# Attention and FFN on one core: conversions behind SiLU in batch 0, and small matmuls gathered behind FFN1 from batch 1 on

## The chip, the cores and the metric

The kernel runs on one core of one Trainium2 chip. The metric is device time in microseconds of one execution, as the median of several. The engines are named as the profile names them: PE is TensorE (matmuls) and PEld its weight loads, DVE is VectorE, ACT is ScalarE, SP issues most of the DMAs.

## What is computed

Eight batches of an attention over 32 memory slots, followed by a feed-forward layer over all 4608 tokens. Cut to what matters:

```
q, k, v: (8, 8, 576, 64)   phi: (8, 8, 576, 32)   w_in: (512, 2048)   w_out: (2048, 512)
a    = exp(phi - max over seq);  a = a / (sum over seq + 1e-9)
k_m  = einsum('bhsm,bhsd->bhmd', a, k);   v_m = the same with v
attn = softmax(q @ k_m^T / 8)                      # over the 32 slots
x    = (attn @ v_m) put together over heads        # (4608, 512)
h    = x @ w_in;   g = h * sigmoid(h);   out = g @ w_out
```

## The kernel before, in words

**Precision.** The large products are made of pairs of a high part and a low part, each of a type that the PE takes quickly (fp32r): high by high, high by low, low by high. So each large product is three matmuls. Splitting a value is a copy to the high part and a subtraction for the low part.

**Order of the algebra.** `attn @ v_m @ w_in` is computed as attn times P, where P = `v_m @ w_in` for one batch (`p_mm`, L560 to L578, matmuls at L570). P is made in four pieces of 512 columns of d_ff (eight of 256 in batch 0), each in the PSUM tile `bg`; `p_split` (L580) then writes its high part on ACT (L584) and its low part on DVE (L586).

**Slots.** For each batch b there are 16 slots, one for each 128 columns of d_ff (`fc`). A slot is: FFN1 (`ffn1`, L590, 12 matmuls at L605) into the PSUM tile `h`; SiLU on ACT (`silu`, L628 for 512 of the 576 tokens, L630 for the other 64, which go to `gleft`); the split of g on DVE (L620 and L622); and FFN2 of the slot before (`ffn2`, 12 matmuls at L642, four tiles of tokens by three parts). The tile `h` has two banks, of which FFN1 uses columns 0 to 287 in each. There is one `h`, so the next FFN1 waits until SiLU has read it. After every second batch the 64 left tokens of two batches go through FFN2 together (`accleft`, `left_step`).

**Attention of the next batch** is done meanwhile, step by step, as events hung on the slots (L672 to L718). Its steps: the maximum of phi (`phi_max`, then `phi_fold`, DVE), the subtraction (`phi_sub`, L294 and L297, DVE), the exponential (`phi_exp`, L301, ACT, with a table load before it and another before the next SiLU); `e_mm` (L315 and L323, small matmuls into `bg`, then reciprocals and `kvn` on DVE and ACT); `e_tr` (the turn: two transposes at L349 and two copies to `kvT`); `s_mm` (the scores in two halves of 288 tokens, small matmuls at L361 into `bg`, turned on DVE at L373); maximum, subtraction, exponential (L395), sum and norm of the scores; `s_back` and `s_low`, which turn them back and split them. In batches 1 to 6 these hang on the slots

```
mx, sub, ex, em, tr, s0, s1, sx, se, ss, sn, sk = 0, 1, 2, 3, 4, 6, 7, 8, 9, 10, 11, 12
```

and P on slots 1, 5 and 9, with the next batch's first piece in slot 14. In a slot the program issues two tiles of FFN2 (six matmuls), then the events of the slot, then the other six, then the events of the half slot (L845 to L848).

**Batch 0** also converts the weights, which arrive as 64-bit words. `w_conv` (L146) has the steps p, c and h on ACT (L166, L168, L174) and s, a and l on DVE (L170, L172, L176); l makes `wo_lo`. The conversions are events of the slots as well. Three buffers hold the raw words.

**What sets the order.** The Tile framework orders the instructions of each engine by priority, which follows the program, and inserts the waits. `in_order` (L98) forces program order on the engines that it names: PE, SP, DVE and ACT in the opening, PE and SP up to the end of batch 0 (`whole`, closed at L836). From batch 1 on no engine is bound by it. In the opening (L729 to L816) batch 0's attention is done by hand, with `keep_warm` matmuls in the gaps; `f_copy` copies scores out of PSUM, whole on ACT or in halves on ACT and DVE, and `f_high` and `f_low` split the result.

Of the kernel before, what the change touches and what calls it, by code (L numbers as in the profile page):

```python
# [10 lines left out]
F32 = mybir.dt.float32  # L11
# [4 lines left out]
AF = mybir.ActivationFunctionType  # L16
# [32 lines left out]
def attn_ffn_kernel(  # L49
# [64 lines left out]
    def bgtile():  # L114
        return ps.tile([P, 2, 512], F32, tag="bg", name="bg", bufs=1)

    raws, cvas = {}, {}

    def w_load(w, part=None, few=False):

# [23 lines left out]
    def w_conv(w, part=None, steps="pcsahl"):  # L146


        kind, j = w
        words = raws[w].bitcast(U32).rearrange("p r (f t) -> p r f t", t=2)  # L150
        low, high = (w_part(words[:, :, :, t], part) for t in range(2))
        r = low.bitcast(I32)
        fc = slice(2 * j, 2 * j + 2) if part is None else slice(2 * j + part, 2 * j + part + 1)
        if kind == "i":
            to = win[:, fc].rearrange("p k r f -> p k (r f)")
            a = to.bitcast(I32)
        else:
            to = high.bitcast(F32)
            if (w, part) not in cvas:
                n, tag = (2, "cva") if part != 1 else (1, "cva1")  # L160
                cvas[w, part] = sb.tile([P, n, DMODEL], I32, tag=tag, name="cva", bufs=1)[:, : 2 if part is None else 1]
            a = cvas[w, part]
        au = a.bitcast(U32)
        for step in steps:
            if step == "p":
                nc.scalar.activation(a.bitcast(F32), high.bitcast(F32), AF.Prelu, scale=2.0**-112, alpha=-(2.0**32))  # L166
            elif step == "c":
                nc.scalar.activation(r, low, AF.Copy, scale=2.0**-29)  # L168
            elif step == "s":
                nc.vector.tensor_scalar(au, au, 3, None, op0=ALU.logical_shift_left)  # L170
            elif step == "a":
                nc.vector.tensor_tensor(to.bitcast(I32), a, r, op=ALU.add)  # L172
            elif kind == "o" and step == "h":
                nc.scalar.activation(wo_hi[:, fc], a.bitcast(F32), AF.Copy)  # L174
            elif kind == "o":
                nc.vector.tensor_tensor(wo_lo[:, fc], to, wo_hi[:, fc], op=ALU.subtract)  # L176

    later = [w for j in range(2, DFF // CW) for w in (("i", j + 1), ("o", j))][:-2] + [("o", DFF // CW - 1)]
    to_load = iter([("i", 1), ("o", 1), ("i", 2)] + later)
# [19 lines left out]
    def banks(b):  # L199
        if b == 0:  # L200
            return [ps.tile([P, 512], F32, tag="acc", name=f"first{i}", bufs=NI) for i in range(2)]
        bg = bgtile()
        return [bg[:, 0], bg[:, 1]]

    def load_phi(b):
        t = sb.tile([P, PHW], F32, tag="att", name=f"phi{b}")
# [99 lines left out]

    def e_mm(b):
        e, er, kvt, kr = (at[b][k] for k in ("e", "er", "kv", "kr"))
        pt = banks(b)
        turns = [(c, p) for c in range(FULLC) for p in range(2)]  # L310
        if b == 0:
            turns.sort(key=lambda t: t[1])
        for c, p in turns:
            for r in range(NR):
                nc.tensor.matmul(  # L315
                    pt[p][M * r : M * (r + 1), :KVW],
                    e[:, p, c, M * r : M * (r + 1)],
                    kvt[c][:, p, r],
                    start=c == 0, stop=False, skip_group_check=True,
                )  # L320
        for r in range(NR):
            for p in range(2):
                nc.tensor.matmul(  # L323
                    pt[p][M * r : M * (r + 1), :KVW],
                    er[rows(p), M * r : M * (r + 1)],
                    kr[rows(p), r],
                    start=False, stop=True, skip_group_check=True,
                )
        rs = [sb.tile([P, 1], F32, tag="rs", name="rs", bufs=2) for p in range(2)]
        for p in range(2):  # L330
            nc.vector.tensor_scalar(rs[p], pt[p][:, 2 * D : KVW], EPS, None, op0=ALU.add)
        for p in range(2):
            nc.vector.reciprocal(rs[p], rs[p])
        for p in range(2):
            src = pt[p][:, : 2 * D].rearrange("p (k d) -> p k d", k=2)
            if p == (b == 0):
                nc.scalar.activation(kvn[:, :, p], src, AF.Copy, scale=rs[p])
            else:
                nc.vector.tensor_scalar(kvn[:, :, p], src, rs[p], None, op0=ALU.mult)  # L339

    def e_tr(b):
        if b > 1:
            bg = bgtile()
            pt = [bg[:, 0, P * kind : P * (kind + 1)] for kind in range(2)]
        else:
            pt = [live["h"][:, kind, HALF : HALF + P] for kind in range(2)]
        t = sb.tile([P, 2, NR, M], F32, tag="kvT", name=f"kvT{b}", bufs=2)
        for kind in range(2):
            nc.tensor.transpose(pt[kind], kvn[:, kind].rearrange("p g d -> p (g d)"), ident)  # L349
        nc.vector.tensor_copy(t[:, 0].rearrange("p r m -> p (r m)"), pt[0])  # L350
        nc.scalar.copy(t[:, 1].rearrange("p r m -> p (r m)"), pt[1])
        at[b]["kvT"] = t

    def s_mm(b, hf):
        if "sc" not in at[b]:
# [269 lines left out]
    def silu(b, fc, h):  # L625
        g32 = sb.tile([P, MAIN], F32, tag="g32", name="g32", bufs=2)
        w = MAIN // 2
        nc.scalar.activation(g32.rearrange("p (h f) -> p h f", h=2), h[:, :, :w], AF.Silu)  # L628
        o = b % 2 * LEFT
        nc.scalar.activation(  # L630
            gleft[:, fc, o : o + LEFT].rearrange("p (h f) -> p h f", h=2), h[:, :, w:HALF], AF.Silu
        )
        return g32

    acc = {}
# [39 lines left out]
        events.setdefault((b, slot), []).append((fn, a))  # L675

    for b in range(B):
        if b == 0:
            for j in range(2, DFF // CW):
                ev(b, 2 * j - 1.5, p_mm, b, j * CW, CW)  # L680
        else:
            for j in range(1, NJ):
                ev(b, 4 * j - 3, p_mm, b, j * JW, JW)
        n = b + 1
        if n == B:
            continue
        at_slot = (4, 5, 6, 7.5, 9, 9.5, 11.5, 11.5, 12, 12.5, 12.5, 13) if b == 0 else (0, 1, 2, 3, 4, 6, 7, 8, 9, 10, 11, 12)
        mx, sub, ex, em, tr, s0, s1, sx, se, ss, sn, sk = at_slot
        ev(b, mx, phi_max, n)
        if n == 1:  # L690
            ev(b, sub, phi_allmax, n, (0, 1), (0,))
            ev(b, sub + 0.5, phi_allmax, n, (0, 1), (1,))
        else:
            for i in range(3):
                ev(b, sub, phi_fold, n, i)
        ev(b, sub + 0.5, phi_sub, n)
        ev(b, ex, phi_exp, n)
        ev(b, em, e_mm, n)
        if n + 1 < B:
            ev(b, 14 if b == 0 else em + 1, load_kv, n + 1)  # L700
        ev(b, tr, e_tr, n)
        ev(b, s0, s_mm, n, 0)
        ev(b, em, load_q, n, 1)
        ev(b, s1, s_mm, n, 1)
        if n + 1 < B:
            ev(b, s1, load_q, n + 1, 0)
        ev(b, sx, s_max, n, ALL)
        ev(b, sx, s_sub, n, ALL)
        ev(b, se, s_exp, n, ALL)
        ev(b, ss, s_sum, n, ALL)  # L710
        ev(b, sn, s_norm, n, ALL)
        ev(b, sk, s_back, n, ALL)
        ev(b, sk, s_low, n, ALL)
        if n + 1 < B:
            ev(b, sk, load_phi, n + 1)
        ev(b, 14, p_mm, n, 0, JW)
# [6 lines left out]
        getattr(mybir.EngineType, e) for e in ("PE", "DVE", "Activation", "SP")  # L723
    )
    whole = ExitStack()
    whole.enter_context(in_order(PE, SP))
    I0, O0, I1 = ("i", 0), ("o", 0), next(to_conv)
    idle = ps.tile([P, 2, 512], F32, tag="h", name="idle", bufs=1)[:, 0]
    with in_order(DVE, ACT) as last:  # L729
# [22 lines left out]
        w_conv(I0, 0, "pc")  # L752
        keep_warm(idle, 3)
        f_tr()
        w_conv(I0, 0, "sa")
        keep_warm(idle, 2)
        f_scores(0)
        f_copy(0)
        spare = ps.tile([P, 512], F32, tag="acc", name="spare", bufs=NI)
        keep_warm(spare, 2)  # L760
        f_turn(0)
        f_scores(1)
        f_max(0)
        f_copy(1, False)
        f_sub(0)
        keep_warm(spare, 3)
        f_turn(1)
# [22 lines left out]
        f_back(1)  # L790
        f_low(0)
        p_split(0, 0, CW, bg, (1,))
        f_high(1)
        f_high(2)
        w_conv(O0, 0, "sh")
        f_low(1)
        f_low(2)
# [36 lines left out]
    for b in range(B):  # L834
        if b == 1:
            whole.close()  # L836
        for fc in range(NFC):
            if b == 0 and fc < 2:
                for part in range(2):
                    for fn, a in events.pop((b, fc + part / 2), []):  # L840
                        fn(*a)
                continue
            h = ffn1(b, fc)
            gs = split(silu(b, fc, h))
            for part in range(2):  # L845
                finish((2 * part, 2 * part + 1))
                for fn, a in events.pop((b, fc + part / 2), []):
                    fn(*a)  # L848
            prev = ("main", b, fc, gs)
        if b % 2:  # L850
            for n in range(NLS):
# [59 lines left out]
```

## Time and profile before

| | us |
|---|---|
| median of 3 runs | 711.29 |
| lowest to highest | 710.79 to 711.51 |
| the profiled execution | 711.12 |
| its span, first to last instruction | 709.3 |
| PE busy in it | 695.2 |
| DVE busy | 367.1 |
| ACT busy | 258.6 |

The profiled execution is one run, recorded by the hardware. A row of the timeline has the start in us from the span's beginning, the length, the engine, the line of the kernel, the operation, output and inputs, and in brackets the idle time of the engine before it with the instruction that ended it. The chain of waits is followed back from the last instruction: each piece is what the end of the span was waiting for at that time. Pieces of the chain follow each other without overlap, so their lengths can be added; the lengths of single matmuls can't, because matmuls overlap.

### The profile page before, as it was taken

The page shows a single profiled execution, that of the slowest core. Times are in us where ns is not written, and L with a number is a line of the kernel's source. Part 1 is how long each engine was busy: PE and PEld are TensorE (multiplying, and loading weights), DVE is VectorE, ACT ScalarE, POOL GpSimd, SP SyncE. Part 2 cuts the span into 40 slices and gives each one's busy share as a digit, 9 for nine tenths or more (in the row PEclk, how much of TensorE's full clock was granted, in tenths as well). Part 3 has the DMA queues.
Part 4 walks back from the last instruction along what each step waited for, and adds up shares of the span by engine and source line. Part 5 has one row for each costly group of instructions (what it writes and reads, how often), then busy time and mean ns, then how long its engine had stood idle before and what let it go on. Part 6 is the DMA issues. An engine that isn't in the chain of part 4 may idle for free.

```text
span 709.3 us, 11575 instructions
## 1 busy us (share of the span) xinstructions
PE 695.2 (98%) x4828; PEld 556.0 (78%) x4828; DVE 367.1 (52%) x666; ACT 258.6 (36%) x455; POOL 0.7 (0%) x6
## 2 busy tenths in 40 slices
PE   8899899999999999999999999999999999999997
PEld 3578678788887788777887778877888878888885
DVE  4898886355353563538246372535635356233322
ACT  3889844233322332424224241423322323222211
POOL 0000000000000000000000000000000000000000
PEclk9999999999999999999999999999999999999999
DMA  9996715311113210232011420131001000010002
GB/s 333 324 339 214 243 50 212 135 68 34 45 31 135 67 34 1 98 131 68 1 60 23 157 71 2 61 135 67 34 26 49 2 1 1 0 61 1 1 1 74
DMA packets 25444, 60.14 MB, mean 85 GB/s; under 512 B 2096, under 2 KB 10416, under 8 KB 25392
## 3 DMA queue, kind: packets, MB, share of 16 engines
q1 hardware_dynamic: 24448, 56.63, 22.6%
q10 hardware_dynamic: 944, 2.77, 1.1%
q8 instruction: 38, 0.62, 0.4%
q14 instruction: 14, 0.11, 0.1%
HBM read 49.95 MB, written 9.44 MB: 84 GB/s over the span
## 4 chain that ended last, share of the span: by engine, by line
PE 79%; ACT 8%; DVE 7%; DMA 3%; issue 2%; ACTq 0%; DVEq 0%
PE acc L642 42%; PE h L605 24%; PE accleft L642 5%; PE bg L570 3%; DMA raw<-in_w_out 2%; PE bg L315 2%; ACT L628 1%; DVE gparts L622 1%; PE bg L361 1%; ACT phi L301 1%; DVE phi L294 1%; ACT g L628 1%; DMA kv<-in_kv 1%; ACT raw L168 1%; ACT cva L166 1%
## 5 line engine op out<-in xcount | busy, mean ns | idle before, releaser
L642 PE MATMUL acc<-wo_hi,gparts 128*128 128x512 f32 x1024 | 352.6, 397 | 0.1
L642 PEld LDWEIGHTS acc<-wo_hi,gparts 128*128 128x128 f32 x1024 | 192.3, 188 | 65.8 <-issue 29.8
L605 PEld LDWEIGHTS h<-aparts,pparts 128*128 128x128 f32 x1524 | 213.6, 188 | 16.9 <-ACT gleft L630 3.1
L605 PE MATMUL h<-aparts,pparts 128*128 128x288 f32 x1524 | 223.6, 296 | 1.7 <-ACT aparts L549 0.7
L642 PE MATMUL acc<-wo_lo,gparts 128*128 128x512 f32 x512 | 201.6, 394 | 0.5 <-DVE wo_lo L176 0.4
L628 ACT ACTIVATE g<-h 128x512 f32<-128x512 f32 x127 | 75.8, 597 | 306.5 <-issue 175.4
L620 DVE CAST gparts<-g 128x512 fp32r<-128x512 f32 x128 | 54.5, 426 | 221.3 <-ACT g L628 220.7
L642 PEld LDWEIGHTS acc<-wo_lo,gparts 128*128 128x128 f32 x512 | 96.2, 188 | 15.8 <-DVE wo_lo L176 1.4
L622 DVE TENSOR_TENSOR gparts<-g,gparts 128x512 fp32r<-128x512 f32 x128 | 88.2, 689 | 10.1
L586 DVE TENSOR_TENSOR pparts<-bg,pparts 128x1024 fp32r<-128x1024 f32 (+1 forms) x36 | 39.5, 1098 | 36.6 <-ACT pparts L584 36.5
L584 ACT ACTIVATE pparts<-bg 128x1024 fp32r<-128x1024 f32 (+1 forms) x36 | 33.3, 926 | 28.6 <-PE bg L570 28.6
L642 PE MATMUL accleft<-wo_hi,gparts 128*128 128x512 f32 x128 | 40.6, 390 | 0.0
L570 PE MATMUL bg<-win,kvT 64*32 64x512 f32 (+1 forms) x576 | 35.8, 554 | 0.4 <-DVE kvn L339 0.4
L642 PEld LDWEIGHTS accleft<-wo_hi,gparts 128*128 128x128 f32 x128 | 24.0, 188 | 4.9
L630 ACT ACTIVATE gleft<-h 128x64 f32<-128x64 f32 x127 | 27.7, 218 | 0.0
L650 ACT ACTIVATE o<-acc 128x512 f32<-128x512 f32 x32 | 19.1, 598 | 21.8 <-PE acc L642 10.7
L642 PE MATMUL accleft<-wo_lo,gparts 128*128 128x512 f32 x64 | 25.0, 390 | 0.0
L628 ACT ACT_TABLE_LOAD x14 | 18.0, 1283 | 8.0 <-PE h L605 7.9
L620 DVE CAST gparts<-gleft 128x512 fp32r<-128x512 f32 x16 | 6.8, 427 | 20.7 <-PE accleft L642 12.2
L570 PEld LDWEIGHTS bg<-win,kvT 64*32 64x32 f32 x576 | 6.6, 105 | 13.7 <-issue 12.1
L168 ACT ACTIVATE raw<-raw 128x1024 int32<-128x1024 uint32 (+1 forms) x16 | 16.7, 1046 | 0.0
L399 DVE TENSOR_REDUCE ssm<-sc 128x36 f32<-128x1152 f32 x7 | 9.5, 1354 | 8.8 <-ACT sc L395 8.8
(133 smaller groups left out, 370.2 us busy)
## 6 DMA issues: line engine op xcount, KB each, us to landing
kv<-in_kv SPq DMA_DIRECT2D x28, 516.0 KB, 5.9
q<-in_q SPq DMA_DIRECT2D x16, 576.0 KB, 3.6
out<-o SPq DMA_DIRECT2D x32, 256.0 KB, 2.1
raw<-in_w_in SPq DMA_DIRECT2D x14, 512.0 KB, 5.8
raw<-in_w_out SPq DMA_DIRECT2D x6, 1024.0 KB, 6.2
phi<-in_phi SPq DMA_DIRECT2D x7, 576.0 KB, 3.6
kv<-in_kv ACTq DMA_DIRECT2D x4, 516.0 KB, 6.4
kr<-in_kv SPq DMA_DIRECT2D x7, 258.0 KB, 7.1
```

What stands on the lines that cost most here:

```text
L168: nc.scalar.activation(r, low, AF.Copy, scale=2.0**-29)
L315: nc.tensor.matmul(pt[p][M * r : M * (r + 1), :KVW], e[:, p, c, M * r : M * (r + 1)], kvt[c][:, p, r], start=c == 0, stop=False, skip_grou ...
L570: nc.tensor.matmul(bg[M * r : M * (r + 1), p, :w].rearrange("p (k f) -> p k f", f=P), kvT[D * p : D * (p + 1), 1, r], win[D * p : D * (p + ...
L584: nc.scalar.activation(hi[:, :, c], bg[:, :, :w], AF.Copy)
L586: nc.vector.tensor_tensor(lo[:, :, c], bg[:, :, :w], hi[:, :, c], op=ALU.subtract)
L605: nc.tensor.matmul(h[:, hf, :HALF], wt[:, p, fs], a[:, p, hf * HALF : (hf + 1) * HALF], start=n[hf] == 0, stop=n[hf] == 5, skip_group_chec ...
L620: nc.vector.tensor_copy(ghi, g32)
L622: nc.vector.tensor_tensor(glo, g32, ghi, op=ALU.subtract)
L628: nc.scalar.activation(g32.rearrange("p (h f) -> p h f", h=2), h[:, :, :w], AF.Silu)
L630: nc.scalar.activation(gleft[:, fc, o : o + LEFT].rearrange("p (h f) -> p h f", h=2), h[:, :, w:HALF], AF.Silu)
L642: nc.tensor.matmul(acc[key], gt[:, cs], wt[:, fc], start=fc == 0 and n == 0, stop=fc == NFC - 1 and n == 2)
L650: nc.scalar.activation(o[:, :w], a[:, :w], AF.Copy)
```

## The change

- **Batch 0.** Each conversion step on ACT gets an ordering edge behind the second SiLU instruction of the slot that was traced last, from slot 2 on. It is no wait between engines; it only fixes ACT's order.
- **From batch 1 on** the events of a slot, P among them, are issued behind FFN1 and ahead of all twelve FFN2 matmuls of the slot before. The steps of attention move to slots 1, 2, 3, 5, 9, 10, 10, 11, 12, 13, 13, 14.
- **Beside h.** For batches from 2 on, `e_mm` and `e_tr` write into the unused columns of `h`, from 288 on, in place of `bg`. The two halves of the scores become one step, `s_all`: 512 columns into `bg`, the last 64 beside `h`.
- **Order.** PE is in program order to the end; ACT is in program order from batch 1 on.
- **Opening.** One conversion's add moves behind the first `f_copy`; the second `f_copy` is done in halves on ACT and DVE; `f_high(2)` comes ahead of `f_high(1)`.

```diff
-    raws, cvas = {}, {}
+    raws, cvas, last_silu = {}, {}, []
...
         for step in steps:
+            i = None
             if step == "p":
-                nc.scalar.activation(a.bitcast(F32), high.bitcast(F32), AF.Prelu, scale=2.0**-112, alpha=-(2.0**32))
+                i = nc.scalar.activation(a.bitcast(F32), high.bitcast(F32), AF.Prelu, scale=2.0**-112, alpha=-(2.0**32))
...
+            if i is not None and last_silu:
+                tc.add_manual_dep(
+                    i.ins,
+                    last_silu[-1].ins.name,
+                    mybir.DependencyInfo(mybir.DependencyClass.NoSync, mybir.DependencyReason.DATA),
+                    reason="behind SiLU",
+                )
...
+    def beside_h(w):
+
+        return [live["h"][:, i, HALF : HALF + w] for i in range(2)]
...
     def e_mm(b):
         e, er, kvt, kr = (at[b][k] for k in ("e", "er", "kv", "kr"))
-        pt = banks(b)
+        pt = banks(b) if b < 2 else beside_h(KVW)
...
     def e_tr(b):
-        if b > 1:
-            bg = bgtile()
-            pt = [bg[:, 0, P * kind : P * (kind + 1)] for kind in range(2)]
-        else:
-            pt = [live["h"][:, kind, HALF : HALF + P] for kind in range(2)]
+        pt = beside_h(P)
...
+    def s_all(b):
+
+        sc = at[b]["sc"] = sb.tile([P, 2, S], F32, tag="att", name=f"sc{b}")
+        bg, left = bgtile(), beside_h(S - 512)
+        kvT = at[b]["kvT"]
+        w = 512 - HALF
+        for hf, f, n in ((0, 0, HALF), (1, 0, w), (1, w, HALF - w)):
+            for r in range(NR):
+                for p in range(2):
+                    to = left[p] if f else bg[:, p, hf * HALF : hf * HALF + n]
+                    nc.tensor.matmul(
+                        to[M * r : M * (r + 1)],
+                        kvT[D * p : D * (p + 1), 0, r],
+                        at[b]["q", hf][D * p : D * (p + 1), r, f : f + n],
+                        start=True, stop=True, skip_group_check=True,
+                    )
+        for p in range(2):
+            nc.vector.transpose(sc[:, p, :512], bg[:, p])
+        for p in range(2):
+            nc.vector.transpose(sc[:, p, 512:], left[p])
...
-        nc.scalar.activation(
+        i = nc.scalar.activation(
             gleft[:, fc, o : o + LEFT].rearrange("p (h f) -> p h f", h=2), h[:, :, w:HALF], AF.Silu
         )
+        if b == 0 and fc > 1:
+            last_silu.append(i)
...
-        at_slot = (4, 5, 6, 7.5, 9, 9.5, 11.5, 11.5, 12, 12.5, 12.5, 13) if b == 0 else (0, 1, 2, 3, 4, 6, 7, 8, 9, 10, 11, 12)
+        at_slot = (4, 5, 6, 7.5, 9, 9.5, 11.5, 11.5, 12, 12.5, 12.5, 13) if b == 0 else (1, 2, 3, 5, 9, 10, 10, 11, 12, 13, 13, 14)
...
-        ev(b, s0, s_mm, n, 0)
         ev(b, em, load_q, n, 1)
-        ev(b, s1, s_mm, n, 1)
+        if n == 1:
+            ev(b, s0, s_mm, n, 0)
+            ev(b, s1, s_mm, n, 1)
+        else:
+            ev(b, s0, s_all, n)
...
-    whole.enter_context(in_order(PE, SP))
+    ctx.enter_context(in_order(PE))
+    whole.enter_context(in_order(SP))
...
-        w_conv(I0, 0, "sa")
+        w_conv(I0, 0, "s")
         keep_warm(idle, 2)
         f_scores(0)
         f_copy(0)
+        w_conv(I0, 0, "a")
...
-        f_copy(1, False)
+        f_copy(1)
...
+        f_high(2)
         f_high(1)
-        f_high(2)
...
         if b == 1:
             whole.close()
+            ctx.enter_context(in_order(ACT))
...
             for part in range(2):
-                finish((2 * part, 2 * part + 1))
+                if b == 0:
+                    finish((2 * part, 2 * part + 1))
                 for fn, a in events.pop((b, fc + part / 2), []):
                     fn(*a)
+            if b:
+                finish(range(NI))
             prev = ("main", b, fc, gs)
```

The steps c and h of a conversion are changed as p is.

More of the change, by code (lines that the diff above doesn't have):

```diff
@@ L164, in w_conv @@
         for step in steps:
+            i = None
             if step == "p":
-                nc.scalar.activation(a.bitcast(F32), high.bitcast(F32), AF.Prelu, scale=2.0**-112, alpha=-(2.0**32))
+                i = nc.scalar.activation(a.bitcast(F32), high.bitcast(F32), AF.Prelu, scale=2.0**-112, alpha=-(2.0**32))
             elif step == "c":
-                nc.scalar.activation(r, low, AF.Copy, scale=2.0**-29)
+                i = nc.scalar.activation(r, low, AF.Copy, scale=2.0**-29)
             elif step == "s":
@@ L173, in w_conv @@
             elif kind == "o" and step == "h":
-                nc.scalar.activation(wo_hi[:, fc], a.bitcast(F32), AF.Copy)
+                i = nc.scalar.activation(wo_hi[:, fc], a.bitcast(F32), AF.Copy)
             elif kind == "o":
                 nc.vector.tensor_tensor(wo_lo[:, fc], to, wo_hi[:, fc], op=ALU.subtract)
+            if i is not None and last_silu:
[5 more added lines that the diff above has]
+                )
     later = [w for j in range(2, DFF // CW) for w in (("i", j + 1), ("o", j))][:-2] + [("o", DFF // CW - 1)]
@@ L677, in attn_ffn_kernel @@
     for b in range(B):
+        n = b + 1
         if b == 0:
@@ L683, in attn_ffn_kernel @@
                 ev(b, 4 * j - 3, p_mm, b, j * JW, JW)
-        n = b + 1
         if n == B:
             continue
-        at_slot = (4, 5, 6, 7.5, 9, 9.5, 11.5, 11.5, 12, 12.5, 12.5, 13) if b == 0 else (0, 1, 2, 3, 4, 6, 7, 8, 9, 10, 11, 12)
+        at_slot = (4, 5, 6, 7.5, 9, 9.5, 11.5, 11.5, 12, 12.5, 12.5, 13) if b == 0 else (1, 2, 3, 5, 9, 10, 10, 11, 12, 13, 13, 14)
         mx, sub, ex, em, tr, s0, s1, sx, se, ss, sn, sk = at_slot
```

## The prediction

> **What bounds the kernel now.** I read the page first, then the chain of waits in order of time through one batch, then sums over stretches, and the timelines of ACT and DVE only where the chain left TensorE.
>
> ```profile
> span 709.3 us, 11575 instructions
> ...
> PE 695.2 (98%) x4828; PEld 556.0 (78%) x4828; DVE 367.1 (52%) x666; ACT 258.6 (36%) x455; POOL 0.7 (0%) x6
> ```
>
> TensorE is busy for all but 14 us of the span. A gain must come out of those 14 us, or out of what a change of the kind of matmul costs inside the busy time. Both show in the chain. This is batch 2 from its slot 2 on; columns are start, length, and what the chain runs over.
>
> ```profile
> 211.20 1.17 ACT phi L301
> ...
> 213.30 1.28 ACT L628
> ...
> 214.59 0.60 ACT g L628
> ...
> 215.36 1.87 PE h L605 x12
> 217.23 1.38 PE acc L642 x6
> 218.61 1.90 PE bg L315 x64
> 220.51 0.38 PE bg L323 x16
> 220.89 1.59 PE acc L642 x6
> ...
> 224.06 1.38 PE acc L642 x6
> 225.44 0.22 PE bg L349 x2
> 225.66 1.39 PE acc L642 x6
> 227.05 1.58 PE h L605 x12
> 228.63 1.39 PE acc L642 x6
> 230.02 1.02 PE bg L570 x16
> 231.04 1.58 PE acc L642 x6
> ...
> 234.21 1.39 PE acc L642 x6
> 235.59 0.65 PE bg L361 x16
> 236.24 1.58 PE acc L642 x6
> ...
> 239.41 1.39 PE acc L642 x6
> ...
> 244.61 2.74 PE acc L642 x12
> ```
>
> From slot 3 on the chain never leaves TensorE. A plain slot is 12 FFN1 matmuls (1.58) and 12 FFN2 (2.74), 4.32 us. A slot with P (L570) has 1.39 + 1.02 + 1.58 in place of 2.74, so P costs 1.25: its own 1.02 and 0.23 of **seam**. Scores (L361) cost 1.39 + 0.65 + 1.58 - 2.74 = 0.88, again 0.23 over their own time; e (L315 and L323) 1.38 + 2.28 + 1.59 - 2.74 = 2.51, again 0.23; the turn (L349) 1.38 + 0.22 + 1.39 - 2.74 = 0.25 in all. The seam lies almost wholly behind the small matmuls: the six FFN2 ahead take 1.39, half of 2.74 and 0.02, those behind take 1.58. One place where the chain leaves TensorE is left, the exponential of phi at the top.
>
> ```profile
> 208.28:287.36 79.08, 79.00 (x564) 63.95 (x563) 39.68 (x76) 26.87 (x50) 0.00 (x0) 1.00 0.19 67
> ```
>
> This stretch is one batch without left work, from a first P to the next. Of its 79.08 us, 16 x 4.32 = 69.12 are plain slots, and 4 x 1.25 + 2.51 + 0.25 + 2 x 0.88 = 9.52 are P, e, turn and scores. The remaining 0.44 is the stall at the exponential: it ran ahead of its slot's SiLU, a table load of 1.28 followed, and SiLU came at 214.59, so that the next FFN1 (215.36) had to wait for h.
>
> **The change, batches 1 to 6.** Slots with small matmuls fall from eight to five: P alone in slot 1; P and e in 5; P and turn in 9; both halves of the scores in 10; the next batch's P in 14. All of it stands behind FFN1 and ahead of twelve unbroken FFN2. The costs: P alone 1.25, twice. P and e 1.02 + 2.28 + one seam 0.23 = 3.53. P and turn I leave at 1.25 + 0.25 = 1.50. The scores now stream 512 columns into bg, which is P's shape (1.02), and 64 columns beside h. That last piece is not in the trace: by columns it is 64/288 of 0.65 = 0.14, by the 16 narrow matmuls of L323 it is 0.38; I take 0.26, near the middle, since neither row has its width, and 1.02 + 0.26 + 0.23 = 1.51. Sum 1.25 + 3.53 + 1.50 + 1.51 + 1.25 = 9.04 against 9.52 + 0.44: 0.92 less per batch if the stall goes, **5.5 us in six batches**. Batch 7 has only three P, at the same price. Entering small matmuls from FFN1 is not in the trace either; from FFN2 it costs 0.02, and the dear side, leaving, costs 0.21 (1.58 against 1.37). I take 0.02, because leaving is what changes the weights that FFN2 must load again, and that side stays as it is; 0.21 is a rival below.
>
> What hides the new waits? e, the turn and the last piece of scores now write into the banks of h, so they wait for SiLU of their own slot, and the next FFN1 waits for whoever reads them. SiLU after an FFN1 that ended at 234.21 by the chain:
>
> ```profile
> 234.30 0.60 ACT L628 ACTIVATE g<-h 128x512 f32<-128x512 f32 x1 [2.13 <-PE h L605]
> 234.80 0.22 ACT L630 ACTIVATE gleft<-h 128x64 f32<-128x64 f32 x1
> ```
>
> It ends at 235.02, 0.81 after FFN1. In slots 5 and 9 P stands in between and in slot 10 the 512 columns, 1.02 each, so the wait is covered by some 0.2; without that cover it would be 0.8 each. On the other side, the tightest slot is 10. DVE there, after an FFN1 that ended at 239.41:
>
> ```profile
> 240.66 0.69 DVE L622 TENSOR_TENSOR gparts<-g,gparts 128x512 fp32r<-128x512 f32 x1
> 241.55 0.85 DVE L373 STREAM_TRANSPOSE sc<-bg 128x288 f32<-128x288 f32 x2 [0.20 <-PE bg L361]
> ```
>
> The split ends 1.94 after FFN1. Two transposes of 288 columns take 0.85; 1152 columns in four take twice that, 1.70, so h is free at about 3.7. The next FFN1 is due at 1.02 + 0.26 + 0.23 + 2.74 = 4.25. Covered, with half a microsecond to spare. e's readers in slot 5 and the turn's copies in slot 9 have the same twelve FFN2 to hide under, and less to do.
>
> ACT in program order puts the exponential behind its slot's SiLU. What is queued behind it is the next SiLU: 0.81 + 1.28 + 1.17 + 1.28 = 4.54 against a slot of 4.32, so that SiLU is 0.22 late. It may be late by 2.74 - 0.81 = 1.93 before FFN1 waits for h. So the 0.44 goes, provided that the subtraction on DVE is done in time; who waits for a late one is first that SiLU and then FFN1. The Trainium skill, in "ScalarE: Activation LUTs", section "What ACT_TABLE_LOAD costs", speaks against this: it counts a drain of about 1380 ns with each load, 2.66 us per switch. The trace has the load at 1.28 and SiLU 0.01 behind it, with no drain to be seen.
>
> The loads on SP's queue move with their steps: kv and the second half of q by two slots, the first half of the next q by three, phi by two, with the phi work one slot later. What each feeds moves as far or stays several slots of 4.32 behind, so I cost them at nothing.
>
> **Batch 0.** Here conversions are held behind their slot's SiLU. The waits of TensorE from slot 2 on:
>
> ```profile
> PE h L349 <- ACT gleft L630: 1.9, 1, 1.9
> ...
> PE bg L361 <- DVE kvT L350: 0.5, 1, 0.5
> ...
> PE acc L642 <- DVE wo_lo L176: 0.4, 1, 0.4
> PE bg L570 <- DVE kvn L339: 0.4, 1, 0.4
> ...
> PE h L605 <- ACT kvT L351: 0.3, 1, 0.3
> ```
>
> ```profile
> 34.58:100.99 66.41, 62.85 (x506) 49.41 (x504) 59.15 (x90) 53.00 (x71) 0.00 (x0) 1.00 0.65 227
> ```
>
> These five are 3.5 of the 3.56 us that TensorE is idle in that stretch. The largest is what the change is about:
>
> ```profile
> 76.01 1.13 ACT L168 ACTIVATE raw<-raw 128x1024 int32<-128x1024 uint32 x1
> 77.03 0.59 ACT L628 ACTIVATE g<-h 128x512 f32<-128x512 f32 x1
> ```
>
> A conversion ran ahead of SiLU, the turn beside h waited 1.9 for it. With SiLU first that goes. The other 1.6 are late copies and conversions on two engines that are busy 59.15 and 53.00 of 66.41 us, and DVE's work is not less; I count half of it, 0.8. **Batch 0 gains 2.7**, between 0 and 3.5, and a loss is possible if conversions come too late (below).
>
> **Opening.**
>
> ```profile
> 14.91 0.38 ACT sT L466
> ...
> 15.31 0.43 DVE sT L468
> ...
> 17.09 0.59 ACT sT L466
> ```
>
> The halves of a copy on two engines ran one behind the other, 0.38 + 0.43, against 0.59 for the whole on ACT; doing the second copy so costs about 0.2. Taking the small high part first lets two matmuls of the first FFN1 start early, 2 x 1.58/12 = 0.26. The add that moves behind the first copy stays hidden under it. Net nothing, within 0.4 either way, which the forecast's own range below takes in.
>
> Sum: 5.5 + 2.7 = 8.2. The profiled execution took 711.12 us (span 709.3), the median of the three runs shown is 711.29, 0.17 more. 711.12 - 8.2 + 0.17 = **703.1 us**.
>
> **The rivals.**
> - All waits of batch 0 go and the narrow scores cost 0.14: 703.1 - 0.8 - 6 x 0.12 = 701.6. For it: the 0.8 hang on the same late SiLU. Against: DVE has little room there. 0.12.
> - Holding conversions back doesn't help batch 0, since they are late instead of SiLU: 703.1 + 2.7 = 705.8. 0.10.
> - Entering from FFN1 costs what leaving costs, 0.19 more at five places in six batches: 5.7, 708.8. 0.08. Together with the rival above it is 711.5, no change. 0.04.
> - h is freed late: in slot 10 an operation like P's low part is queued on DVE ahead of the four transposes.
>
> ```profile
> 213.31 1.23 DVE L586 TENSOR_TENSOR pparts<-bg,pparts 128x1024 fp32r<-128x1024 f32 x1 [2.15 <-ACT pparts L584]
> ```
>
>   1.23 less the half microsecond to spare leaves 0.7 of waiting, 4.2 in six batches: 707.3. For it: DVE's order is left to the scheduler. Against: P's low part belongs to a slot before and should be done. 0.06.
> - The other side: the weights' low parts. FFN2 already waits once for wo_lo. From slot 3 on six more output conversions stand behind SiLU, with DVE work at their end. If each of those FFN2 waits x, the time is 703.1 + 2.7 + 6x; it is slower than before from x = 0.9 on, and an ACT operation of the kind above (1.13) queued ahead of each gives 712.6. For it: DVE is busy for 89% of that stretch. Against: ACT has 13 us free in it. 0.06, a third of it with x small enough to be no change.
> - ACT stands still before each table load, in program order as it did not before. A stop as long as the load itself, 1.28, twice in a slot with an exponential, makes SiLU 0.22 + 2.56 = 2.78 late, 0.85 over what it may; two such slots in six batches lose 10.2: 713.3. Against it stands the 0.01 behind the load. 0.02. With the drain of the skill's page it would be some 12.6 and 715.7, an estimate.
>
> **How the numbers follow.** The forecast has 0.52; its own range is 702 to 705. The range 700.5 to 709.0 takes in every case up to the seam's 708.8 and leaves out 0.12. A measurement of this kernel can tell about 0.2%, 1.4 us. Faster by more: 0.52 + 0.12 + 0.10 + 0.08 + 0.06 = 0.88. Same: 0.04 + 0.02 = 0.06. Slower: 0.04 + 0.02 = 0.06.
>
> **What would show it.** A batch without left work should take 78.2 us from first P to first P; the chain there should stay on TensorE through the slots with exponentials; e should start where P ends with no wait for gleft; FFN2 should stand in unbroken twelves. In batch 0 the turn's wait of 1.9 should be gone and TensorE idle under 1 us. Wrong would be: a wait of FFN1 for the transposes or copies beside h, of e for gleft, more than one wait for wo_lo, or twelve FFN2 behind small matmuls that take longer than 2.74 + 0.21.

## The result: 705.12 us, and the profile after

| | before | after |
|---|---|---|
| median, us (4 runs each, taken together) | 711.4 | 705.12 |
| lowest to highest | 710.79 to 711.77 | 704.6 to 705.4 |
| the profiled execution | 711.12 | 704.6 |
| its span | 709.3 | 702.8 |

The ratio of after to before is 0.9912, with a 95% interval of 0.9895 to 0.9929. The kernel is faster by 6.3 us. 703.1 us was forecast; the measured time is 2.0 us more than that, 0.1 above the forecast's own 702 to 705 and inside the wide range.

In the code after the change the lines are others: FFN1 is L634, FFN2 L673, P L599 with its split at L613 and L615, e L327 and L335, the turn L357, the new scores L372, the old ones (batch 0) L390, SiLU L657 and L659, the split of g L649 and L651, and the steps of the conversion p, c, h on ACT L167, L169, L175 and s, a, l on DVE L171, L173, L177. The head of the page:

```profile
span 702.8 us, 11778 instructions
...
PE 690.1 (98%) x4924; PEld 562.7 (80%) x4924; DVE 366.1 (52%) x667; ACT 258.7 (37%) x455; POOL 0.7 (0%) x6
```

PE has 5.1 us less of busy time with 96 more matmuls, and the span outside PE's busy time went from 14.1 to 12.7 us. Read alone, this would say that little waiting went away; but matmuls that wait in PE's pipeline count as busy (batch 2 before had 79.00 of 79.08 us busy, its stall of 0.44 included). The chain of waits through batch 2 shows what it is (start, length, what the chain runs over):

```profile
206.16 1.02 PE bg L599 x16
207.18 2.95 PE acc L673 x12
...
223.10 1.57 PE h L634 x12
224.68 1.02 PE bg L599 x16
225.70 1.90 PE h L327 x64
227.59 0.38 PE h L335 x16
227.97 2.97 PE acc L673 x12
...
245.50 1.02 PE bg L599 x16
246.52 0.37 PE h L357 x2
246.88 2.76 PE acc L673 x12
249.64 1.58 PE h L634 x12
251.22 1.02 PE bg L372 x32
252.24 0.18 PE h L372 x16
252.43 2.94 PE acc L673 x12
```

The chain never leaves PE in this batch. FFN1 ahead of small matmuls takes the same 1.57 or 1.58 as anywhere. The twelve FFN2 behind them take 2.94 to 2.97 in place of 2.74, so there is one seam of some 0.20 to 0.23 per group, and there are five groups in place of eight. The group that ends in the turn is the exception: the FFN2 behind it take 2.76. Its two transposes take 0.37 behind P, where they took 0.22 between FFN2 before, so most of that group's seam stands ahead of or in the transposes. The same batch, from first P to first P, in sums by stretch (length, then busy time and count of PE, PEld, DVE, ACT):

```profile
206.09:284.05 77.96, 77.96 (x580) 64.99 (x579) 39.49 (x75) 26.86 (x49) 0.00 (x0) 1.00 0.20 67
```

It was 79.08 and is 77.96. Both kernels have 69.12 of plain slots in it; the remaining 9.96 (by the prediction's count 9.52 of small matmuls and 0.44 of stall) became 8.84.

In batch 0 the waits of PE from slot 2 to the FFN1 of slot 14 (waiter, what it waited for, total, times, longest) and the sum of that stretch are now

```profile
PE h L634 <- ACT gleft L659: 1.2, 1, 1.2
PE acc L673 <- DVE wo_lo L177: 0.6, 2, 0.4
PE acc L673 <- DVE gparts L651: 0.5, 1, 0.5
PE acc L673 <- DVE gparts L649: 0.4, 1, 0.4
```

```profile
35.16:101.21 66.05, 63.42 (x505) 49.22 (x504) 57.96 (x86) 53.05 (x71) 0.00 (x0) 1.00 0.65 229
```

Four of the five waits of before are gone, the turn's 1.9 among them. The one for `wo_lo` in slot 3 is still there, with a second of 0.2 in slot 7, and three others are new, for SiLU and for the split. The stretch took 66.41 and takes 66.05. Inside it there are a gain and a loss. From the FFN1 of slot 2 to that of slot 10 it was 34.58 to 81.11, 46.53 us, and is 35.16 to 78.62, 43.46 us: 3.07 less, nearly all of it in slot 9. From there to the FFN1 of slot 14 it was 19.88 and is 22.59: 2.71 more, all of it from the FFN1 of slot 13 on. The chain through that end, after the change:

```profile
93.41 1.22 DVE wo_lo L177
94.63 1.27 DVE sc L420
...
96.75 0.69 DVE gparts L651
97.43 0.62 DVE cva L171
...
98.07 1.06 ACT wo_hi L175
...
99.15 1.28 ACT L657
...
100.45 0.60 ACT g L657
...
101.21 1.85 PE h L634 x12
```

Read from the bottom: the FFN1 of slot 14 waits for SiLU of slot 13, which waits for a table load, which stands behind a conversion (L175, wo_hi). That conversion waits for its shift on DVE (L171), and DVE was late with it because the split of g (L649, L651) and before it the score work (L420) and the end of an earlier conversion (L177) were in its way. Before the change the last conversion was done at 89.2 us (its L176 on DVE), and the chain over these slots ran on PE alone.

So the profiled execution's 6.5 us are: opening and slots 0 and 1 +0.58 (the FFN1 of slot 2 starts at 35.16, it was 34.58), slots 2 to 9 -3.07, slots 10 to 13 +2.71, and all from there to the end -6.7.

### The profile page after: what moved, and what is told of

The parts are those of the page before. It is cut to its first block, busy times and chain, and to the rows that moved or that the text cites. A ratio compares the mean times of both kernels' runs of the same rounds, so it can differ in the third digit from the quotient of the medians.

```text
span 702.8 us, 11778 instructions
## 1 busy us (share of the span) xinstructions
PE 690.1 (98%) x4924; PEld 562.7 (80%) x4924; DVE 366.1 (52%) x667; ACT 258.7 (37%) x455; POOL 0.7 (0%) x6
## 4 chain that ended last, share of the span: by engine, by line
PE 85%; DVE 1%; ACT 0%; issue 0%; ACTq 0%
PE acc L673 46%; PE h L634 26%; PE accleft L673 6%; PE bg L599 4%; PE h L327 2%; PE bg L372 1%; PE h L335 0%; PE h L357 0%; ACT L657 0%; DVE sc L420 0%; DVE wo_lo L177 0%; DVE raw L173 0%; PE h L372 0%; ACT wo_hi L175 0%; DVE sc L402 0%
## 5 line engine op out<-in xcount | busy, mean ns | idle before, releaser
L673 PE MATMUL acc<-wo_hi,gparts 128*128 128x512 f32 x1024 | 342.1, 395 | 0.9 <-DVE gparts L651 0.5
L673 PEld LDWEIGHTS acc<-wo_hi,gparts 128*128 128x128 f32 x1024 | 192.2, 188 | 53.9 <-issue 6.6
L634 PEld LDWEIGHTS h<-aparts,pparts 128*128 128x128 f32 x1524 | 214.0, 188 | 15.0 <-issue 2.5
L634 PE MATMUL h<-aparts,pparts 128*128 128x288 f32 x1524 | 223.1, 295 | 1.5 <-ACT gleft L659 1.2
L657 ACT ACTIVATE g<-h 128x512 f32<-128x512 f32 x127 | 76.0, 598 | 348.7 <-PE h L634 179.8
L673 PE MATMUL acc<-wo_lo,gparts 128*128 128x512 f32 x512 | 201.0, 393 | 0.6 <-DVE wo_lo L177 0.6
L649 DVE CAST gparts<-g 128x512 fp32r<-128x512 f32 x128 | 54.5, 426 | 261.3 <-ACT g L657 261.2
L673 PEld LDWEIGHTS acc<-wo_lo,gparts 128*128 128x128 f32 x512 | 96.1, 188 | 18.3 <-DVE wo_lo L177 1.9
L651 DVE TENSOR_TENSOR gparts<-g,gparts 128x512 fp32r<-128x512 f32 x128 | 88.2, 689 | 10.6 <-DVE gparts L649 0.5
L615 DVE TENSOR_TENSOR pparts<-bg,pparts 128x1024 fp32r<-128x1024 f32 (+1 forms) x36 | 39.7, 1102 | 5.2 <-ACT pparts L613 4.8
L673 PE MATMUL accleft<-wo_hi,gparts 128*128 128x512 f32 x128 | 40.6, 390 | 0.0
L613 ACT ACTIVATE pparts<-bg 128x1024 fp32r<-128x1024 f32 (+1 forms) x36 | 33.6, 932 | 14.2 <-PE bg L599 14.1
L599 PE MATMUL bg<-win,kvT 64*32 64x512 f32 (+1 forms) x576 | 35.8, 554 | 0.0
L673 PEld LDWEIGHTS accleft<-wo_hi,gparts 128*128 128x128 f32 x128 | 24.0, 188 | 4.9
L659 ACT ACTIVATE gleft<-h 128x64 f32<-128x64 f32 x127 | 27.8, 219 | 0.0
L673 PE MATMUL accleft<-wo_lo,gparts 128*128 128x512 f32 x64 | 24.9, 390 | 0.0
L657 ACT ACT_TABLE_LOAD x14 | 18.0, 1283 | 14.3 <-issue 13.8
L649 DVE CAST gparts<-gleft 128x512 fp32r<-128x512 f32 x16 | 6.8, 427 | 20.7 <-PE accleft L673 12.2
L169 ACT ACTIVATE raw<-raw 128x1024 int32<-128x1024 uint32 (+1 forms) x16 | 16.7, 1041 | 0.0
L327 PEld LDWEIGHTS h<-kv,phi 128*32 128x32 f32 x384 | 10.2, 110 | 5.0 <-ACT gleft L659 5.0
L673 PEld LDWEIGHTS accleft<-wo_lo,gparts 128*128 128x128 f32 x64 | 12.0, 188 | 2.4
```

The costliest lines, as they stand in the source:

```text
L169: i = nc.scalar.activation(r, low, AF.Copy, scale=2.0**-29)
L327: nc.tensor.matmul(pt[p][M * r : M * (r + 1), :KVW], e[:, p, c, M * r : M * (r + 1)], kvt[c][:, p, r], start=c == 0, stop=False, skip_grou ...
L599: nc.tensor.matmul(bg[M * r : M * (r + 1), p, :w].rearrange("p (k f) -> p k f", f=P), kvT[D * p : D * (p + 1), 1, r], win[D * p : D * (p + ...
L613: nc.scalar.activation(hi[:, :, c], bg[:, :, :w], AF.Copy)
L615: nc.vector.tensor_tensor(lo[:, :, c], bg[:, :, :w], hi[:, :, c], op=ALU.subtract)
L634: nc.tensor.matmul(h[:, hf, :HALF], wt[:, p, fs], a[:, p, hf * HALF : (hf + 1) * HALF], start=n[hf] == 0, stop=n[hf] == 5, skip_group_chec ...
```

## The experiments

The theory after these profiles: the whole gain comes from batches 1 to 7, partly from fewer seams and partly from the stall that went, and batch 0 gives back what it wins, because the last conversions now stand in the slots that also have the score work. The rivals were that batch 0 does contribute, that the steady batches gain by ACT's order alone, and, within batch 0, that ACT or else DVE is what runs late. The kernel before ran beside each group of experiments on the same chip; its medians there are 711.72, 711.73 and 711.89 (711.4 beside the changed kernel), and each ratio is to its own. The changed kernel was not run again beside them, so a difference to its 705.12 is uncertain by the 0.5 us by which these medians differ.

**Batches 1 to 7 alone.** The changed kernel without the ordering edges of the conversions and with the opening of before.

```diff
-        if b == 0 and fc > 1:
-            last_silu.append(i)
...
-        w_conv(I0, 0, "s")
+        w_conv(I0, 0, "sa")
...
-        w_conv(I0, 0, "a")
...
-        f_copy(1)
+        f_copy(1, False)
...
-        f_high(2)
         f_high(1)
+        f_high(2)
```

> The changed kernel without its conversion edges and without the three edits of the opening: only batches 1 to 6 are changed. Theory (five places with small matmuls instead of eight, and no stall at the exponential, make the whole gain): the batch without left work takes 78.0 us from first P to first P as in the changed kernel (79.08 before), six batches gain 6.8 us, the time is about 704.6 against 711.4, ratio 0.990. Rival (the gain in batch 0 is real and large, batches 1 to 6 bring only what I forecast, 5.5): 705.9, ratio 0.992.

Measured: 704.95 us (704.36 to 705.93), ratio 0.9904 (0.9889 to 0.9919). Without these two parts of the change the kernel is as fast as with them; the ratio is the theory's 0.990, and the rival's 0.992 lies just outside the interval. Its waits in batch 0 are again of the kind of before:

```profile
PE h L357 <- ACT gleft L659: 1.6, 1, 1.6
PE bg L599 <- DVE kvn L351: 1.1, 1, 1.1
```

**The edges alone**, in the kernel before.

```diff
+            if i is not None and last_silu:
+                tc.add_manual_dep(i.ins, last_silu[-1].ins.name, ...)
...
+        if b == 0 and fc > 1:
+            last_silu.append(i)
```

> The kernel before with the conversion edges of batch 0 alone. Theory (the edges gain 3.1 us in slots 2 to 9, the turn's wait of 1.9 among them, and lose 2.7 in slots 12 and 13, where the last conversion, the exponential and its two table loads now meet): 0.4 less, 711.0, ratio 0.999; the wait of the turn for gleft is gone and a new wait of over 1 us stands in slots 12 to 13. Rival (the loss in slots 12 and 13 comes from something else in the change, the edges alone keep their gain): 708.3, ratio 0.996.

Measured: 711.18 us (710.96 to 711.79), ratio 0.9992 (0.9984 to 1.0001), so the rival's 708.3 is out. The turn's wait is gone, and the new waits have the lengths that they have in the changed kernel:

```profile
PE h L613 <- ACT gleft L638: 1.2, 1, 1.2
...
PE acc L652 <- DVE gparts L630: 0.5, 1, 0.5
PE acc L652 <- DVE gparts L628: 0.4, 1, 0.4
```

Its chain there has the same steps as the changed kernel's: the subtraction of the scores, the split, the shift and the high part of the last conversion, a table load, SiLU and the FFN1 of slot 14 at 100.64. So gain and loss both belong to the edges, and together they come to nothing that can be measured.

**The opening alone**, in the kernel before: the inverse of the lines on `w_conv`, `f_copy` and `f_high` above.

> The kernel before with the three edits of the opening alone. Theory (halves of a copy on two engines run one behind the other): the second turn starts 0.3 to 0.4 us later, the time rises by 0.3 us, ratio 1.0004. Rival (the later start of the opening in the profile of the changed kernel was chance, the early high part saves 0.26): 0.3 less.

Measured: 711.76 us (710.84 to 712.84), ratio 1.0004 (0.9995 to 1.0013), which can't be told from no change, nor the theory from its rival. Its trace shows where a small loss would come from. The second turn of the opening waits for the left piece of the copy, which ACT now does behind the half on DVE:

```profile
18.17 0.66 PE L480 MATMUL firstu<-ident,sT 128*128 128x128 f32 x4 [0.48 <-ACT sleft L469]
```

In the kernel before it started at 17.85, behind the same left piece. The first FFN1 does start earlier (26.98, before 27.04), but it takes 2.21 where it took 1.87, and the FFN1 of slot 2 comes at 34.86, 0.28 later than before.

**ACT's order alone**, in the kernel before from batch 1 on.

```diff
             whole.close()
+            ctx.enter_context(in_order(ACT))
```

> The kernel before with ACT in program order from batch 1 on, and nothing else: slots, places and order of TensorE as before. Theory (the 0.36 to 0.44 us per batch at the exponential of phi are lost because it ran ahead of its slot's SiLU): a batch without left work takes 78.7 instead of 79.08, six batches gain 2.2 to 2.6, 709.0, ratio 0.997. Rival (the stall hangs on the slot distance of the phi work, not on ACT's order): 711.4, ratio 1.000. Second rival (order on ACT makes most of the gain of batches 1 to 6): 705 to 706.

Measured: 709.4 us (709.18 to 709.71), ratio 0.997 (0.9958 to 0.9981). The slot behind the exponential is now a plain one in its chain:

```profile
212.67 2.74 PE acc L642 x12
215.41 1.58 PE h L605 x12
```

Before, that FFN1 had waited for h and taken 1.87. The theory's 709.0 held, and the second rival is out. From the P of slot 1 in batch 1 to that in batch 7 its trace has 505.30 us where the kernel before has 507.20. So of the steady batches' 6.7 us some 2 are this stall (1.9 by the traces, 2.3 by the medians). The other 4.4 to 4.8 are the groups.

**The new slots without ACT's order**: the changed kernel less that one line.

```diff
-            ctx.enter_context(in_order(ACT))
```

> The changed kernel without ACT in program order from batch 1 on; every event stays where the change put it. Theory: the move of the events and the order of ACT are separate gains. Holding ACT in order took 0.39 us a batch off the kernel before, because ACT no longer meets an exponential of the next batch ahead of a SiLU that is ready; with the changed slots and a planner that may again put the exponential first, the stall comes back once a batch, 6 x 0.36 to 0.44 = 2.2 to 2.6 us: 705.1 + 2.4 = 707.5 us, ratio to the kernel before 0.994. Rival: in the new slots the exponential falls after the SiLU whether ordered or not, so nothing comes back: 705.1 us, 0.991.

Measured: 714.04 us (713.29 to 714.49), ratio 1.0033 (1.002 to 1.0045). Neither number held: it is slower than the kernel before, and 9 us slower than the changed kernel. Without the order the Tile framework puts the exponential of the scores ahead of the SiLUs of slots 11 and 12, behind which it stands with the order; the h of slot 11 is ready. Here is ACT in batch 2:

```profile
253.36 1.28 ACT L424 ACT_TABLE_LOAD   x1
258.79 1.17 ACT L424 ACTIVATE sc<-sc 128x1152 f32<-128x1152 f32 x1 [4.14 <-DVE sc L420]
259.98 1.28 ACT L657 ACT_TABLE_LOAD   x1
261.27 0.60 ACT L657 ACTIVATE g<-h 128x512 f32<-128x512 f32 x1
```

and PE:

```profile
262.03 1.62 PEld L634 LDWEIGHTS h<-aparts,pparts 128*128 128x128 f32 x12 [1.44 <-ACT gleft L659]
```

The exponential stands at the head of ACT's queue and waits 4.14 us for its subtraction on DVE. Behind it waits SiLU, and behind that FFN1. A batch from first P to first P takes 79.44 (207.47 to 286.91), 1.48 more than with the order; six of them are 8.9 us. The expected 0.4 a batch was taken from the place of the exponential before; here another exponential stands ahead of a SiLU that is ready, and it waits longer. Moving the steps and ordering ACT are not two gains to be added: the move needs the order.

**Small matmuls between the halves of FFN2 again**, as before the change, with everything else as after it.

```diff
             for part in range(2):
-                if b == 0:
-                    finish((2 * part, 2 * part + 1))
+                finish((2 * part, 2 * part + 1))
                 for fn, a in events.pop((b, fc + part / 2), []):
                     fn(*a)
-            if b:
-                finish(range(NI))
```

> The changed kernel, but in batches 1 to 6 the events stand between the two halves of FFN2, as they did before; slots, what lies beside h, and ACT's order stay as changed. Theory (the place behind FFN1 leaves whoever reads h all twelve FFN2 to hide under; seams cost nearly the same in either place): seams 0.04 more at five places, and in slot 10 the next FFN1 is due 1.4 us sooner after the scores and waits 0.3 to 0.4 for the transposes: 0.5 to 0.6 per batch, 3.3 in six, 708.4. Rival (the place behind FFN1 is what saves the seams): 5 x 0.23 per batch, 7 us, 712. Second rival (the place doesn't matter): 705.1 to 706.3.

Measured: 708.11 us (707.48 to 708.24), ratio 0.995 (0.9933 to 0.9966), 3.0 above the changed kernel, near the theory's 708.4. Its chain in the slot of the scores:

```profile
252.92 1.02 PE bg L372 x32
253.94 0.11 PE h L372 x16
254.05 1.62 PE acc L673 x6
255.67 0.10 issue
255.77 1.83 PE h L634 x12
```

With only six FFN2 behind the scores, h is not yet free when the next FFN1 is due: the FFN2 end at 255.67, and FFN1 runs 0.10 late and 0.25 long, 0.35 of the 0.5 us per batch. The place behind FFN1 pays because twelve FFN2 then hide the readers of h.

**No cover for e and the turn**: e in slot 6 and the turn in slot 8, where no P stands between FFN1 and them.

```diff
-else (1, 2, 3, 5, 9, 10, 10, 11, 12, 13, 13, 14)
+else (1, 2, 3, 6, 8, 10, 10, 11, 12, 13, 13, 14)
```

> The changed kernel with e in slot 6 and the turn in slot 8, where no P stands ahead of them, in place of slots 5 and 9. Theory (e and the turn beside h wait for SiLU of their slot, and P's 1.02 hides it): each waits 0.9 to 1.0 for gleft and pays a seam of its own, 2.2 per batch, 13 us in six batches, 718. Rival (e and the turn don't have to wait for SiLU, or SiLU is early enough): only the seams, 0.3 per batch, 707.

Measured: 718.41 us (717.92 to 718.83), ratio 1.0093 (1.0078 to 1.0108). The chain of waits ahead of e:

```profile
231.49 1.59 PE h L634 x12
...
233.75 0.12 ACT gleft L659
...
233.92 1.97 PE h L327 x64
```

From the end of FFN1 (231.49 + 1.59 = 233.08) to e (233.92) there are 0.84 of waiting for SiLU, and as much again ahead of the turn. With two seams of 0.2 more in the batch, that makes 2.1 a batch and 13 us in six. The P ahead of e is what pays for putting e beside h.

**The end of batch 0, ACT's part**: the edges stop at slot 10, so that the last conversions may run ahead again.

```diff
-        if b == 0 and fc > 1:
+        if b == 0 and 1 < fc < 11:
             last_silu.append(i)
```

> The changed kernel, but the conversion edges stop at slot 10: the last three conversions may run as soon as SiLU of slot 10 is done. Theory (the last conversion, held behind SiLU of slot 12, meets the exponential and its two table loads there, and SiLU of slot 13 comes 4 us late): the waits of TensorE in slots 12 and 13 go, 2.7 us less than the changed kernel's 705.1, 702.4, ratio to the kernel before 0.987. Rival (DVE is what is late there, the score work of batch 1 and two conversions at once): the waits stay, 705.1.

Measured: 704.0 us (703.32 to 704.15), ratio 0.9889 (0.9875 to 0.9904). This is 1.1 better than the changed kernel, where 2.7 were expected; the intervals of the two ratios overlap. Both theories hold in part: the long wait for SiLU is mostly gone, but PE now waits for the split.

```profile
97.08 0.30 PEld L673 LDWEIGHTS acc<-wo_hi,gparts 128*128 128x128 f32 x2 [0.67 <-DVE gparts L651]
99.86 1.62 PEld L634 LDWEIGHTS h<-aparts,pparts 128*128 128x128 f32 x12 [0.64 <-ACT gleft L659]
102.84 0.30 PEld L673 LDWEIGHTS acc<-wo_hi,gparts 128*128 128x128 f32 x2 [1.10 <-DVE gparts L651]
```

The same with the opening of before:

> The same, with the opening of the kernel before. Theory (the opening's edits cost 0.3): 702.1, ratio 0.9867. Rival (they cost nothing that can be measured): as the run with edges to slot 10.

Measured: 703.62 us (703.52 to 703.87), ratio 0.9886 (0.9872 to 0.9901). The 0.4 between the two is what the opening was held to cost, but the intervals overlap.

**The end of batch 0, DVE's part.** In the chain of the kernel with edges to slot 10, the maximum of the scores, their subtraction and their normalization (1.26 or 1.27 each) stand around the splits. So, with the edges to slot 10 and the opening of before, the score work goes half a slot later (its last step a whole slot), and each step of it on DVE behind the split of its slot:

```diff
+    def behind_split(b, i):
+        if b == 1 and last_split:
+            tc.add_manual_dep(i.ins, last_split[-1].ins.name, ...)
...
-            nc.vector.tensor_tensor(glo, g32, ghi, op=ALU.subtract)
+            last_split.append(nc.vector.tensor_tensor(glo, g32, ghi, op=ALU.subtract))
...
-(4, 5, 6, 7.5, 9, 9.5, 11.5, 11.5, 12, 12.5, 12.5, 13) if b == 0
+(4, 5, 6, 7.5, 9, 9.5, 11.5, 12, 12.5, 13, 13, 14) if b == 0
```

> The changed kernel with the opening of before, the conversions held behind their slot's SiLU up to slot 10 only, and in batch 0 the score work of the next batch half a slot later, each of its DVE steps behind the split of the slot it is in. Theory: what is left of the wait in slots 12 and 13 of batch 0 is DVE, which has the maximum and the subtraction (1.34 and 1.35 us) and the multiplication (1.35 us) ahead of or inside a split that PE waits for: 0.67, 0.64 and 1.10 us. With the split first, of these 2.4 us at least 1 goes, the rest may move to the SiLU of slot 14 behind the later exponential: 702.6 us, range 701.6 to 703.2, ratio 0.987. Rival: DVE is full in these slots whatever its order, so the wait only moves to slots 14 and 15 or to the first FFN1 of batch 1: 703.6 us, 0.9886, as without the edges.

Measured: 701.8 us (701.28 to 702.73), ratio 0.9861 (0.9846 to 0.9876). From slot 2 on the waits of PE in batch 0 are now

```profile
PE acc L686 <- DVE wo_lo L177: 0.6, 2, 0.4
```

The waits for the split and for SiLU are gone, and none has come in their place: the rival, that the wait only moves to slots 14 and 15 or to batch 1, is refuted. Which of the two did it, the later slots or the place behind the split, was not run apart. Last, the same with a single edge, behind the SiLU of slot 9:

```diff
-        if b == 0 and 1 < fc < 11:
+        if b == 0 and fc == 9:
             last_silu.append(i)
```

> As the run with the score work behind the split, but the conversions are held behind one SiLU alone, that of slot 9, and run ahead in all other slots. Theory: the hold earns its gain at the turn of slots 9 and 10 alone (1.9 of 3.07 us in slots 2 to 9), so some of the rest, up to 1.1 us, is given back by conversions ahead of SiLUs in slots 2 to 8, while the last conversions finish somewhat earlier: 703 us, 0.9878. Rival: the 3.07 us hang on this one edge: 702.6 us, no difference from the run with edges to slot 10.

Measured: 701.26 us (701.08 to 701.64), ratio 0.9853 (0.9838 to 0.9868). The other edges are not needed. It was expected to give back up to 1.1 us in slots 2 to 8; it gave back nothing that shows. In the traces its slots 2 to 9 take 43.05 us and those of the run ahead of it 43.50, and its second wait for `wo_lo` is gone. Both versions beat the changed kernel, by 3.3 and 3.9 us; the two can't be told apart.

## Why the prediction was right, and where it was not

The time came out in the range, near the forecast's own, partly by luck: the steady batches gained 1.2 us more than forecast, and batch 0 gained 2.3 less.

- **Batches 1 to 6, predicted -5.5: measured -6.7 (six times 1.12), a little more.** The mechanism is as described, but its two parts were sized wrongly, one each way. The stall was taken as the 0.44 that remained of the batch, of which the order alone takes off 0.30 in its trace; the groups were to save 0.48 a batch and saved the other 0.82. The terms are these: P alone 1.02 + 2.95 - 2.74 = 1.23 (predicted 1.25); P and e 1.02 + 1.90 + 0.38 + 2.97 - 2.74 = 3.53 (3.53; the 2.97 is 0.02 over the length that the prediction gave as a sign of being wrong); P and turn 1.02 + 0.37 + 2.76 - 2.74 = 1.41 (1.50, with a whole seam between P and the turn); scores 1.02 + 0.18 + 2.94 - 2.74 = 1.40 (1.51). The last piece of the scores took 0.18, near its lower bound of 0.14 by columns, not 0.26: time goes by columns there, not by the count of matmuls. The same is seen ahead of it, where 32 matmuls, half of 288 columns and half of 224, take the 1.02 of P's 16 matmuls of 512. The 0.38 of the narrow matmuls of e was no bound for it: they have 129 columns, twice as many. Entering from FFN1 costs nothing in the chain, so the rival with 0.19 at each entry is refuted.
- **The stall at the exponential, predicted to go: it went**, by the order alone (709.4 us). The Trainium skill, in "ScalarE: Activation LUTs", section "What ACT_TABLE_LOAD costs", adds a drain of about 1380 ns to each load of about 1283 ns. The 1283 agrees with the 1.28 of this trace; the drain is not to be seen here, since a load at 99.15 is followed by its SiLU at 100.45. The sum for the late SiLU had something else wrong. It let the second table load follow the exponential; in the trace that load waits until FFN1 has ended (at 265.61 in slot 13 of batch 2), 1.12 us behind the exponential. In the kernel before, seven such loads waited 7.9 us in all for FFN1 in the same way. After the change:

```profile
265.68 1.28 ACT L657 ACT_TABLE_LOAD   x1 [1.12 <-issue]
```

  So SiLU starts at 266.97, some 1.3 later than in a plain slot, not 0.22. The stall went even so, because 1.3 is still under the 1.93 that SiLU may be late.
- **The covers, predicted at 0.2 and at half a microsecond, are as thin as that.** In slot 5 SiLU ends by 225.48 and e starts at 225.70, in the first two rows here; in slot 10 the last transpose beside h, the third row, ends at 254.65, and the next FFN1 starts at 255.37 by the chain. Timelines of ACT and DVE after the change:

```profile
224.76 0.60 ACT L657 ACTIVATE g<-h 128x512 f32<-128x512 f32 x1 [2.33 <-issue]
225.26 0.22 ACT L659 ACTIVATE gleft<-h 128x64 f32<-128x64 f32 x1
```

```profile
254.31 0.34 DVE L381 STREAM_TRANSPOSE sc<-h 128x64 f32<-128x64 f32 x2
```

  Taking each cover away cost what was said: 0.84 for each wait of e and the turn, and a late FFN1 behind the scores. The rival of an operation on DVE ahead of the transposes did not come about: in batch 2 the first transpose follows the split at once.
- **Batch 0, predicted -2.7: measured -0.36.** This step failed. Its first half was right and was even too small: the turn's 1.9 went, and so did 1.2 of the other 1.6, the wait for `kvn` in slot 8 and the two for `kvT` behind the turn, 3.07 in all. They went with the single edge behind the SiLU of slot 9 too. The 0.4 for `wo_lo` stayed. What was missing is the second half, that the conversions held back must be done somewhere. The rival "holding conversions back doesn't help batch 0, since they are late instead of SiLU", 705.8 us at a chance of 0.10, is the one that came true. The prediction had seen that ACT has room in that stretch (13 us), and 3.9 us of it did lie in slots 12 and 13 (ACT was busy 5.64 of the 9.49 us from 91.50 to 100.99). But a conversion goes back and forth between ACT and DVE, and there its shift on DVE came behind the score work and the split, and the next table load on ACT came behind the conversion. A sum of one engine's idle time says nothing about work that has to pass through two. The rival with wo_lo late in six FFN2 did not come true; there are two such waits, of 0.6 together, one more than the prediction allowed. PE is idle for 2.6 us of the stretch (66.05 less 63.42), where under 1 was predicted.
- **Opening, predicted 0, within 0.4 either way.** The profiled execution has +0.58 up to slot 2, of which 0.2 stand ahead of the copy that was changed (the scores there start at 16.49, before 16.27). The run of the opening alone has +0.28 up to slot 2 in its trace, but +0.04 us against its before in the medians (ratio 1.0004), and there are 0.4 between two runs that differ by it. The 0.26 that an early start of the first FFN1 was to gain did not come: it starts early and takes as much longer. A small loss is likely and is not shown by the times.

6.7 + 0.36 - 0.58 make the 6.5 us of the profiled executions. The forecast was 8.2.

## What to carry to other kernels

An ordering edge that holds work back moves that work; look at the slots where it will land, engine by engine, before counting what it frees. Where a big unit's buffer is shared, put small matmuls where one unit's work covers the wait for the buffer and the next unit's covers its release, and check both covers by their lengths. If steps are moved to later slots under a planner, fix the order of the engine that serves the critical wait too: here the move alone cost 2 us, the order alone gained 2, and both together gained over 6.

## What the runs showed of the hardware

- The time that a group of small matmuls costs beyond its own comes at its end, and per group, not per matmul: 0.20 to 0.23 for groups of 16 to 96 small matmuls of 64x32 and 128x32 weights. The Trainium skill, in "TensorEngine Tiling (Array Packing)", section "Key Properties", says that a change of the tiling mode drains TensorE, without a figure. For leaving, these traces are in line with that and give one, though no run here tells a drain from the reloading of FFN2's weights. Entering shows no cost in the chain, and neither do the changes inside the group of slot 5, from 64x32 (P) to 128x32 and back to 64x32 (e): its pieces take the 1.02, 1.90 and 0.38 that they take apart.
- A group that ends in two transposes with whole 128x128 weights leaves only 0.02 behind it (2.76 against 2.74), but behind P the transposes themselves take 0.37 and not 0.22; together 0.17, a little under the 0.21 behind P alone.
- The halves of a copy out of one PSUM tile, one on ACT and one on DVE, ran one behind the other in the opening before the change, 0.38 and 0.43 against 0.59 for the whole on ACT. The DVE half waited for the ACT half; that the two could not have run at once is not shown.
